# Routing logits of all units by fp32 matmuls from unsplit rows

## The chip, the cores and the metric

The kernel runs on one core of one Trainium2 chip. The metric is the device time of one execution in microseconds (us). Engines are called PE (TensorE, the matmul engine), DVE (VectorE), ACT (ScalarE), POOL (GpSimd) and SP (SyncE, which here issues most of the DMAs).

## The reference

The input x has 8 sequences of 2880 tokens with 192 channels, all fp32. Eight heads of 24 channels each get a causal convolution of 7 taps, whose weights are a softmax over the taps. The 23040 rows that come out go through a mixture of experts in two levels:

```
g_logits = x @ w_group                 # 192 x 4
g_idx = argmax(g_logits);  g_w = softmax(g_logits)[g_idx]
e_logits = x @ w_expert[g_idx]         # 192 x 4 in each group
e_idx = argmax(e_logits);  e_w = softmax(e_logits)[e_idx]
out = g_w * e_w * (relu(x @ w1[g_idx, e_idx]) @ w2[g_idx, e_idx])   # 192 -> 1024 -> 192
```

So each row goes to one of 16 experts, and 20 logits a row (4 for the groups and 16 for the experts) decide which.

## The kernel before

**Units.** The rows are routed in 18 units of 4, 8 or 12 blocks of 120 rows: units 0 to 5 have 4, 8, 12, 8, 8 and 8 blocks, units 6 to 17 have 12 each. A unit is a generator, `unit(u)`, which yields after each small step. `step()` moves one of the two or three live units on by a step, and `gaps(u)` says how many steps lie between the transposes, the logits and the transposes back. A unit does, in this order:

- the convolution as matmuls with a banded matrix (L421), copied from PSUM by ACT into `xc` (L430);
- for each group q of four blocks, transposes of `xc` into PSUM on PE, channels 0 to 127 in `turn_a` (L440) and channels 128 to 191 in `turn_b` (L455), and their copies into the tiles `tah` and `tb`, 480 columns wide;
- `logits()` (L477): matmuls whose moving operand is such a tile and whose stationary is a slice of a zero-padded table of router weights. The groups q write to different rows of one PSUM tile, so all accumulate into it, with all M rows of it each time;
- `logits_back()` (L487): four transposes back, so that rows stand in partitions again, and the copy into `lg`;
- softmax, argmax and prefix sums on DVE (L526 to L556), and the store of the convolved rows to DRAM;
- after `rest` more steps, counts by two small matmuls (L567, L568), places in the experts' lists on DVE (L571 to L607: `ohl`, `ohr`, `ohv`), after up to eight more steps (`LISTLAG`) the list matmuls (L622), and a scatter of row numbers to a table in DRAM (L634).

**Two ways to the logits.** PE multiplies fp32 exactly, or takes fp32r operands, which are fp32 rounded by the engine that writes them. `UF = 7` chooses: units 0 to 6 use fp32 (the table `wrf`, two matmuls for each q, `tah` with 128 channels and `tb` with 64, M = 20 x the number of groups). Units 7 to 17 use fp32r: ACT writes `tah` and the upper half of `tb` rounded (L447, L460), DVE writes what the rounding left into `tal` and into the lower half of `tb` (L448, L461), the table `wrz` holds rounded weights and their rests side by side, so that M is 40 x the number of groups, and there are three matmuls for each q. After the transposes back ACT copies one half and DVE adds the other (L495, L496).

**Experts.** After five units the first portion of the lists is opened, and the experts' slots of 256 rows begin: a gather of rows (L706), transposes (L719, L720), `hidden` (L737, w1, with fp32r operands and their rests), relu into `hh` and `hl` (L742 ACT, L743 DVE), `back` (L755, L759, w2) into two PSUM banks of the pool `po`, and `finish`: the scaling into `ys` (L806 ACT, L807 DVE), which frees the banks, and a scatter into the output (L810). Weights come from DRAM through SP's queue (L655 to L659) into a ring of three buffers and are split into rounded part and rest by ACT and DVE (L671 to L687). The first portion has one slot for each of the 16 experts, the two others two, and 18 tail slots end the program. The steps of units 5 to 17 run between the matmuls of the slots, at a rate worked out from what must be routed before the next portion opens; so the later units stand further apart.

**Order.** A scheduler sets each engine's final order from this program order, except where `keep_in_program_order` holds it. Engines work in order: what waits on DVE holds up what stands behind it there. PSUM has eight banks: three in `pm`, three in `ph`, two in `po`; once the slots run, units use `pm` alone.

Of the kernel before, what the change touches and what calls it, by code (L numbers as in the profile page):

```python
# [35 lines left out]
def conv_moe_kernel(  # L36
# [98 lines left out]
    UF = 7  # L135
# [206 lines left out]
    W2 = 2 * NL  # L342
    QS = UB // QB
    WA = (QS - 1) * W2
    wrz = const.tile([P, 3, WA + QS * W2], F32R, name="wrz")
# [3 lines left out]
    def router_weights():  # L349
        nc.gpsimd.memset(wrf, 0.0)  # L350
        nc.gpsimd.tensor_copy(out=wrf[:, :, WF:WF + NL], in_=wr)
        nc.vector.memset(wrz.bitcast(F32), 0.0)
        nc.vector.tensor_copy(out=wrz[:, 0:2, WA:WA + NL], in_=wr)
        nc.vector.tensor_copy(out=wrz[:, 2, WA:WA + NL], in_=wr[:, 0, :])
        nc.vector.tensor_tensor(
            out=wrz[:, 0:2, WA + NL:WA + W2], in0=wr, in1=wrz[:, 0:2, WA:WA + NL].bitcast(F32), op=ALU.subtract)

# [18 lines left out]
    def unit(u, pre=None):  # L376
# [57 lines left out]
        WQ2 = NL if u < UF else W2  # L434
        parts, lgts = {}, []

        def turn_a(q):
            psa = bank("t")
            for i in range(QB):
                nc.tensor.transpose(psa[:, i * BT:(i + 1) * BT], xc[0:BT, q * QB + i, 0:P], ident[0:BT, 0:BT])  # L440
            tah = pa.tile([P, QN], F32R, name="tah", bufs=QS)
            tal = pa.tile([P, QN], F32R, name="tal", bufs=QS)
            if u < UF:
                nc.scalar.activation(out=tah.bitcast(F32), in_=psa[:, 0:QN], func=AF.Copy)
                parts[q] = (tah.bitcast(F32),)
                return
            nc.scalar.activation(out=tah, in_=psa[:, 0:QN], func=AF.Copy)  # L447
            nc.vector.tensor_tensor(out=tal, in0=psa[:, 0:QN], in1=tah.bitcast(F32), op=ALU.subtract)  # L448
            parts[q] = tah, tal

        def turn_b(q):
            psb = bank("t")
            tb = pa.tile([P, QN], F32R, name="tb", bufs=QS)
            for i in range(QB):
                nc.tensor.transpose(psb[0:D2, i * BT:(i + 1) * BT], xc[0:BT, q * QB + i, P:D], ident[0:BT, 0:BT])  # L455
            if u < UF:
                nc.scalar.activation(out=tb[0:D2].bitcast(F32), in_=psb[0:D2, 0:QN], func=AF.Copy)
                parts[q] += (tb.bitcast(F32),)
                return
            nc.scalar.activation(out=tb[0:D2], in_=psb[0:D2, 0:QN], func=AF.Copy)  # L460
            nc.vector.tensor_tensor(out=tb[D2:P], in0=psb[0:D2, 0:QN], in1=tb[0:D2].bitcast(F32), op=ALU.subtract)  # L461
            parts[q] += (tb,)

        def logits():

            lt = bank("l")
            M = NQ * WQ2
            if u < UF:
                ops = [
                    (wrf[0:n, k, WF - q * NL:WF - q * NL + M], parts[q][k][0:n])  # L470
                    for q in range(NQ) for k, n in enumerate((P, D2))]
            else:
                ops = [
                    (wrz[:, (0, 2, 1)[k], WA - q * W2:WA - q * W2 + M], parts[q][k])
                    for q in range(NQ) for k in range(3)]
# [7 lines left out]
        def logits_back():  # L483
            lgp = bank("l")
            M = NQ * WQ2
# [4 lines left out]
            lgv = lgp[0:BT, 0:QB * M].rearrange("p (i q n) -> p i q n", i=QB, n=WQ2)  # L490
            lgq = lg[0:BT].rearrange("p (q i) n -> p i q n", i=QB)
            if u < UF:
                nc.scalar.activation(out=lgq, in_=lgv, func=AF.Copy)
                return
            nc.scalar.activation(out=lgq, in_=lgv[:, :, :, NL:], func=AF.Copy)  # L495
            nc.vector.tensor_tensor(out=lgq, in0=lgq, in1=lgv[:, :, :, 0:NL], op=ALU.add)  # L496
# [795 lines left out]
```

## Time and profile before

| | us |
|---|---|
| median of 3 runs | 1213.55 (1210.65 to 1219.6) |
| the profiled execution | 1214.05, its span 1212.2 |
| busy: PE | 1129.5 (93%) |
| busy: DVE | 862.2 (71%) |
| busy: ACT | 696.7 (57%) |
| busy: POOL | 495.0 (41%) |
| chain that ended last | PE 66%, DVE 16%, DMA 8%, issue 4%, ACT 4% |

A row of a group names line, engine, operation, output<-inputs, shapes, count, then busy us and mean ns of one, then the idle time just before it on its engine and what ended it. A row of the timeline has the start, the duration (of a merged piece with its count), and in brackets the idle time before and its releaser. A row of the stages has the stretch, its length, the busy us of PE, of PE's weight loads, of DVE, ACT and POOL, then the granted PE clock as a share of full speed, the DMA share and GB/s. Matmul records overlap, so the time that a matmul takes in a stream is read from start to start. An fp32 matmul has two records, an fp32r one has one.

### The profile page before, as it was taken

What the parts mean: (1) busy time and instruction counts of PE and PEld (TensorE: products, weight loads), DVE (VectorE), ACT (ScalarE), POOL (GpSimd) and SP (SyncE); (2) the same over time, 40 slices, a digit from 0 to 9 for tenths busy, and PEclk for the clock granted to TensorE, in tenths of its full rate; (3) what the DMA queues carried; (4) which work ended last, traced back from release to release, by engine and by line L of the source; (5) the groups of instructions that cost most, each with busy time, mean ns of one, the idle gap of its engine ahead of it and who ended that gap; (6) DMA issues with size and microseconds to landing.
All of it is one profiled execution on the core that took longest, in us unless ns stands there. A gap on an engine that the chain in (4) does not pass through costs nothing.

```text
span 1212.2 us, 23621 instructions
## 1 busy us (share of the span) xinstructions
PE 1129.5 (93%) x8219; PEld 1062.1 (88%) x8219; DVE 862.2 (71%) x1835; ACT 696.7 (57%) x1362; POOL 495.0 (41%) x441
## 2 busy tenths in 40 slices
PE   5878899989899999999999999999999999999994
PEld 4444788888899999999999899999999999999994
DVE  4556998898687868676778556666666566687882
ACT  4544566665556556555644445555556555687782
POOL 2003033323334435433343434444444444577771
PEclk9989999999899999999999999999999999999997
DMA  8756588777967464543635657544444456389960
GB/s 210 215 141 153 148 223 191 204 191 195 222 192 213 118 166 137 156 119 104 162 108 145 87 137 212 153 125 137 136 129 136 129 150 162 99 247 258 263 169 15
DMA packets 169628, 195.62 MB, mean 161 GB/s; under 512 B 24932, under 2 KB 146749, under 8 KB 169502
## 3 DMA queue, kind: packets, MB, share of 16 engines
q1 hardware_dynamic: 127454, 140.43, 43.6%
q0 software_dynamic: 18720, 35.83, 10.7%
q10 hardware_dynamic: 23328, 17.80, 6.0%
q8 instruction: 65, 1.06, 0.4%
q14 instruction: 61, 0.50, 0.2%
HBM read 158.80 MB, written 36.58 MB: 161 GB/s over the span
## 4 chain that ended last, share of the span: by engine, by line
PE 66%; DVE 16%; DMA 8%; issue 4%; ACT 4%; SPq 1%; POOL 0%; POOLq 0%; DVEq 0%; ACTq 0%
PE ph L737 28%; PE po L755 17%; PE po L759 8%; PE pm L421 3%; DVE hl L743 3%; DVE ohl L599 2%; PE pm L477 2%; DMA out<-ys,idpt 2%; DMA xin<-in_x 2%; DVE cw L687 1%; DMA raw<-in_moe_w 1%; PE pm L719 1%; PE pm L720 1%; DMA xcd<-xc 1%; DVE tb L461 1%
## 5 line engine op out<-in xcount | busy, mean ns | idle before, releaser
L755 PE MATMUL po<-cw,hh 128*128 128x384 f32 x1424 | 445.8, 371 | 12.2 <-DVE ys L807 12.0
L737 PE MATMUL ph<-xa,ah 128*128 128x256 f32 x1424 | 390.0, 296 | 4.7 <-DVE hl L743 4.6
L810 POOL DMA_INDIRECT out<-ys,idp x160 | 169.2, 1058 | 474.5 <-DVE ys L807 415.4
L759 PE MATMUL po<-cw,hl 128*128 128x192 f32 x1424 | 357.8, 251 | 0.0
L743 DVE SCALAR_TENSOR_TENSOR hl<-ph,hh 128x512 fp32r<-128x512 f32 x356 | 241.2, 685 | 139.8 <-ACT hh L742 137.9
L742 ACT ACTIVATE hh<-ph 128x512 fp32r<-128x512 f32 x356 | 210.6, 593 | 204.1 <-PE ph L737 194.2
L755 PEld LDWEIGHTS po<-cw,hh 128*128 128x128 f32 x1424 | 269.7, 189 | 17.3 <-DVE ys L807 13.9
L737 PEld LDWEIGHTS ph<-xa,ah 128*128 128x128 f32 x1424 | 272.9, 192 | 7.4 <-DVE hl L743 5.0
L759 PEld LDWEIGHTS po<-cw,hl 128*128 128x128 f32 x1424 | 273.8, 192 | 2.0
L706 POOL DMA_INDIRECT xg<-xcd,idp x160 | 186.4, 1165 | 54.6 <-issue 25.9
L737 PE MATMUL ph<-xb,bh 128*128 128x256 f32 x712 | 202.8, 285 | 0.0
L737 PE MATMUL ph<-xb,bl 128*128 128x256 f32 x712 | 202.5, 284 | 0.0
L737 PE MATMUL ph<-xa,al 128*128 128x256 f32 x712 | 202.2, 284 | 0.0
L737 PEld LDWEIGHTS ph<-xa,al 128*128 128x128 f32 x712 | 137.5, 193 | 1.9
L737 PEld LDWEIGHTS ph<-xb,bl 128*128 128x128 f32 x712 | 137.7, 193 | 0.0
L737 PEld LDWEIGHTS ph<-xb,bh 128*128 128x128 f32 x712 | 137.2, 193 | 0.1
L687 DVE TENSOR_TENSOR cw<-rawc,cw 128x768 fp32r<-128x768 f32 x114 | 105.5, 954 | 16.1 <-ACT cw L686 14.0
L725 ACT ACTIVATE xb<-pm 64x256 fp32r<-64x256 f32 x98 | 36.0, 368 | 111.2 <-DVE xa L722 111.2
L672 DVE TENSOR_TENSOR al<-raw,ah 128x1024 fp32r<-128x1024 f32 x57 | 70.6, 1239 | 33.4 <-ACT ah L671 33.4
L686 ACT ACTIVATE cw<-rawc 128x768 fp32r<-128x768 f32 x114 | 90.8, 836 | 3.2 <-DMA rawc<-in_moe_w 3.2
L807 DVE SCALAR_TENSOR_TENSOR ys<-po,xg,ys 128x192 f32<-128x192 f32 x187 | 76.1, 416 | 23.1 <-ACT ys L806 16.7
L806 ACT ACTIVATE ys<-po,xg 128x192 f32<-128x192 f32 x187 | 76.1, 418 | 21.3 <-PE po L759 12.7
(258 smaller groups left out, 1601.4 us busy)
## 6 DMA issues: line engine op xcount, KB each, us to landing
rawc<-in_moe_w SPq DMA_DIRECT2D x114, 384.0 KB
raw<-in_moe_w SPq DMA_DIRECT2D x57, 512.0 KB
raw<-in_moe_w SPq DMA_DIRECT2D x114, 256.0 KB
xcd<-xc ACTq DMA_DIRECT2D x13, 1085.6 KB
xin<-in_x SPq DMA_DIRECT2D x7, 1134.0 KB
xc<-in_moe_w SPq DMA_DIRECT2D x18, 384.0 KB
xin<-in_x SPq DMA_DIRECT2D x6, 1039.5 KB
xin<-in_moe_w SPq DMA_DIRECT2D x9, 512.0 KB
```

The lines of the kernel that those rows point to most:

```text
L672: eng.get(k, nc.vector).tensor_tensor(out=al, in0=ra, in1=ah.bitcast(F32), op=ALU.subtract)
L686: pin(PINW, nc.scalar.activation(out=cw[:, fs, 0, :], in_=rc[k - 2], func=AF.Copy))
L687: eng.get(k, nc.vector).tensor_tensor(out=cw[:, fs, 1, :], in0=rc[k - 2], in1=cw[:, fs, 0, :].bitcast(F32), op=ALU.subtract,)
L706: nc.gpsimd.indirect_dma_start(out=xs[:, t, :], out_offset=None, in_=xcd[0:known, :], in_offset=bass.IndirectOffsetOnAxis(ap=ids[:, t, 0:1 ...
L737: nc.tensor.matmul(out=hp[:, j], lhsT=wgt[:, fs], rhs=xx, start=i == 0, stop=i == len(ops) - 1)
L742: nc.scalar.activation(out=hh, in_=hp, func=AF.Relu)
L743: nc.vector.scalar_tensor_tensor(out=hl, in0=hp, scalar=0.0, in1=hh.bitcast(F32), op0=ALU.max, op1=ALU.subtract,)
L755: nc.tensor.matmul(out=oo[t][:, 0:2 * D], lhsT=hh[:, j, ts], rhs=cw[:, f].rearrange("p a d -> p (a d)"), start=f == 0, stop=False,)
L759: nc.tensor.matmul(out=oo[t][:, 0:D], lhsT=hl[:, j, ts], rhs=cw[:, f, 0, :], start=False, stop=f == NF - 1,)
L806: nc.scalar.activation(out=ys[:, t, :], in_=oo[t][:, D:2 * D], func=AF.Copy, scale=g)
L807: nc.vector.scalar_tensor_tensor(out=ys[:, t, :], in0=oo[t][:, 0:D], scalar=g, in1=ys[:, t, :], op0=ALU.mult, op1=ALU.add,)
L810: nc.gpsimd.indirect_dma_start(out=outviews[nscat[0] % len(outviews)], out_offset=bass.IndirectOffsetOnAxis(ap=ids[:, t, 0:1].bitcast(U32) ...
```

## The change

All units take the fp32 way. `UF`, the table `wrz`, the tiles `tal` and the lower half of `tb` are gone, and so are the rests on DVE and the addition after the transposes back. For units 7 to 17 `logits()` makes six matmuls of fp32 with M = 60 in place of nine of fp32r with M = 120. Nothing else in the source differs.

```diff
--- before.py
+++ after.py
@@ -132,7 +132,6 @@
     FRU = 99
     FRE = nc.gpsimd
     FRH = 0
-    UF = 7
     UG = [0, 5, 3, 6, 1, 4, 0, 8, 0, 5, 3, 6, 0, 4, 4, 7, 0, 5, 4, 6, 2, 6, 5, 10]
     SK = [8, 8, 6, 11, 10, 9, 9]
     KPRE = [5, 6, 16, 33, 35, 47, 63, 68, 79]
@@ -339,21 +338,13 @@
         nc.vector.tensor_scalar(out=band[0:R, h], in0=band[0:R, h], scalar1=wr_[0:R, h:h + 1], scalar2=None, op0=ALU.mult)
 
 
-    W2 = 2 * NL
     QS = UB // QB
-    WA = (QS - 1) * W2
-    wrz = const.tile([P, 3, WA + QS * W2], F32R, name="wrz")
     WF = (QS - 1) * NL
     wrf = const.tile([P, 2, WF + QS * NL], F32, name="wrf")
 
     def router_weights():
         nc.gpsimd.memset(wrf, 0.0)
         nc.gpsimd.tensor_copy(out=wrf[:, :, WF:WF + NL], in_=wr)
-        nc.vector.memset(wrz.bitcast(F32), 0.0)
-        nc.vector.tensor_copy(out=wrz[:, 0:2, WA:WA + NL], in_=wr)
-        nc.vector.tensor_copy(out=wrz[:, 2, WA:WA + NL], in_=wr[:, 0, :])
-        nc.vector.tensor_tensor(
-            out=wrz[:, 0:2, WA + NL:WA + W2], in0=wr, in1=wrz[:, 0:2, WA:WA + NL].bitcast(F32), op=ALU.subtract)
 
 
     posn = const.tile([P, N // BT], I32, name="posn")
@@ -431,48 +422,31 @@
         lg = rt.tile([P, UB, NL], F32, name="lg")[:, 0:nb]
         QN = QB * BT
         NQ = nb // QB
-        WQ2 = NL if u < UF else W2
         parts, lgts = {}, []
 
         def turn_a(q):
             psa = bank("t")
             for i in range(QB):
                 nc.tensor.transpose(psa[:, i * BT:(i + 1) * BT], xc[0:BT, q * QB + i, 0:P], ident[0:BT, 0:BT])
-            tah = pa.tile([P, QN], F32R, name="tah", bufs=QS)
-            tal = pa.tile([P, QN], F32R, name="tal", bufs=QS)
-            if u < UF:
-                nc.scalar.activation(out=tah.bitcast(F32), in_=psa[:, 0:QN], func=AF.Copy)
-                parts[q] = (tah.bitcast(F32),)
-                return
+            tah = pa.tile([P, QN], F32, name="tah", bufs=QS)
             nc.scalar.activation(out=tah, in_=psa[:, 0:QN], func=AF.Copy)
-            nc.vector.tensor_tensor(out=tal, in0=psa[:, 0:QN], in1=tah.bitcast(F32), op=ALU.subtract)
-            parts[q] = tah, tal
+            parts[q] = (tah,)
 
         def turn_b(q):
             psb = bank("t")
-            tb = pa.tile([P, QN], F32R, name="tb", bufs=QS)
+            tb = pa.tile([P, QN], F32, name="tb", bufs=QS)
             for i in range(QB):
                 nc.tensor.transpose(psb[0:D2, i * BT:(i + 1) * BT], xc[0:BT, q * QB + i, P:D], ident[0:BT, 0:BT])
-            if u < UF:
-                nc.scalar.activation(out=tb[0:D2].bitcast(F32), in_=psb[0:D2, 0:QN], func=AF.Copy)
-                parts[q] += (tb.bitcast(F32),)
-                return
             nc.scalar.activation(out=tb[0:D2], in_=psb[0:D2, 0:QN], func=AF.Copy)
-            nc.vector.tensor_tensor(out=tb[D2:P], in0=psb[0:D2, 0:QN], in1=tb[0:D2].bitcast(F32), op=ALU.subtract)
             parts[q] += (tb,)
 
         def logits():
 
             lt = bank("l")
-            M = NQ * WQ2
-            if u < UF:
-                ops = [
-                    (wrf[0:n, k, WF - q * NL:WF - q * NL + M], parts[q][k][0:n])
-                    for q in range(NQ) for k, n in enumerate((P, D2))]
-            else:
-                ops = [
-                    (wrz[:, (0, 2, 1)[k], WA - q * W2:WA - q * W2 + M], parts[q][k])
-                    for q in range(NQ) for k in range(3)]
+            M = NQ * NL
+            ops = [
+                (wrf[0:n, k, WF - q * NL:WF - q * NL + M], parts[q][k][0:n])
+                for q in range(NQ) for k, n in enumerate((P, D2))]
             for i, (wgt, xx) in enumerate(ops):
                 nc.tensor.matmul(
                     out=lt[0:M, 0:QN], lhsT=wgt, rhs=xx, start=i == 0, stop=i == len(ops) - 1)
@@ -482,18 +456,14 @@
 
         def logits_back():
             lgp = bank("l")
-            M = NQ * WQ2
+            M = NQ * NL
             for i in range(QB):
                 nc.tensor.transpose(
                     lgp[0:BT, i * M:(i + 1) * M], lgts[0][0:M, i * BT:(i + 1) * BT], ident[0:M, 0:M],
                 )
-            lgv = lgp[0:BT, 0:QB * M].rearrange("p (i q n) -> p i q n", i=QB, n=WQ2)
+            lgv = lgp[0:BT, 0:QB * M].rearrange("p (i q n) -> p i q n", i=QB, n=NL)
             lgq = lg[0:BT].rearrange("p (q i) n -> p i q n", i=QB)
-            if u < UF:
-                nc.scalar.activation(out=lgq, in_=lgv, func=AF.Copy)
-                return
-            nc.scalar.activation(out=lgq, in_=lgv[:, :, :, NL:], func=AF.Copy)
-            nc.vector.tensor_tensor(out=lgq, in0=lgq, in1=lgv[:, :, :, 0:NL], op=ALU.add)
+            nc.scalar.activation(out=lgq, in_=lgv, func=AF.Copy)
 
         ga, gl, gb, rest = gaps(u)
         events = {}
```

The scheduler's order around it moves a little. On PE, here the logits of unit 9 (`tah`, `tb`, `tal` its transposed tiles, `wrz` and `wrf` the tables), which stand between `back` of one slot and `hidden` of the next. Before:

```order
L759 MATMUL po_1871<-cw_1908,hl_2070 128x192
L477 MATMUL pm_2244<-tah_2033,wrz_200 120x480
L477 MATMUL pm_2244<-tal_2034,wrz_200 120x480
L477 MATMUL pm_2244<-tb_2057,wrz_200 120x480
...
L477 MATMUL pm_2244<-tb_2193,wrz_200 120x480
L737 MATMUL ph_2267<-xa_1978,ah_2046 128x256
...
L737 MATMUL ph_2267<-xb_1979,bl_2074 128x256
L622 LDWEIGHTS ohl_2140
L622 MATMUL pm_2273<-ohv_2142,ohl_2140 128x64
```

Now (lines of the changed kernel: L451 is the logits' matmul, L592 the list's, L707 and L729 those of `hidden` and `back`):

```order
L729 MATMUL po_1826<-cw_1863,hl_2021 128x192
L451 MATMUL pm_2189<-tah_1987,wrf_200 60x480
L451 MATMUL pm_2189<-tb_2009,wrf_200 60x480
...
L451 MATMUL pm_2189<-tb_2139,wrf_200 60x480
L707 MATMUL ph_2209<-xa_1932,ah_1998 128x256
...
L707 MATMUL ph_2209<-xb_1933,bl_2025 128x256
L592 LDWEIGHTS ohl_2088
L592 MATMUL pm_2215<-ohv_2090,ohl_2088 128x64
```

Six matmuls stand where nine stood, and the list of unit 8 still comes after the first five matmuls of `hidden`.

On DVE, at unit 7, the first one that was split. `off` to `pos` begin the list work of unit 5, `mx` and `dd` the softmax of unit 6. Before:

```order
L556 RECIPROCAL xc_858<-se_1191 120x8
L448 TENSOR_TENSOR tal_1227<-pm_1221,tah_1226 128x480
L461 TENSOR_TENSOR tb_1231<-po_1230,tb_1231 64x480
L448 TENSOR_TENSOR tal_1253<-pm_1247,tah_1252 128x480
L461 TENSOR_TENSOR tb_1257<-ph_1256,tb_1257 64x480
L448 TENSOR_TENSOR tal_1276<-po_1270,tah_1275 128x480
L461 TENSOR_TENSOR tb_1280<-pm_1279,tb_1280 64x480
L571 TENSOR_TENSOR off_1290<-ph_1287,eoff_159 128x16
```

Now:

```order
L526 RECIPROCAL xc_843<-se_1171 120x8
L496 TENSOR_REDUCE mx_1296<-lg_1022 120x60
L541 TENSOR_TENSOR off_1261<-ph_1258,eoff_159 128x16
L543 TENSOR_REDUCE mx16_1263<-ph_1258 128x1
L547 TENSOR_TENSOR endr_140<-ph_1258,endr_140 128x16
```

The six rests are gone, and the first reduction of the softmax stands ahead of the list work.

On SP, where the second portion's lists are loaded (`idp1`, sixteen loads, one for each expert; `raw` and `rawc` are weights). Before, from the tenth load on:

```order
L1042 DMA idp1_4122<-idtab_88 128x4
L659 DMA rawc_3618<-in_moe_w2 128x4x192
L659 DMA rawc_3781<-in_moe_w2 128x4x192
L1042 REGISTER_ALU
...
L656 DMA raw_3780<-in_moe_w1 64x1024
L657 DMA raw_3780<-in_moe_w1 64x1024
L655 DMA raw_3961<-in_moe_w1 128x1024
```

Now, from the last of the sixteen on:

```order
L1012 DMA idp1_4021<-idtab_88 128x4
L629 DMA rawc_3521<-in_moe_w2 128x4x192
L629 DMA rawc_3683<-in_moe_w2 128x4x192
L626 DMA raw_3682<-in_moe_w1 64x1024
L627 DMA raw_3682<-in_moe_w1 64x1024
L625 DMA raw_3863<-in_moe_w1 128x1024
```

The weights that stood after ten loads, and after twelve, now stand after all sixteen.

## The prediction

> **What bounds the kernel now.** I read the busy time by stages first, then the waits of TensorE (PE), then single rows. The stages are cut where the kind of work changes: routing alone up to 107 us, the hand-over, expert slots with dense routing, a stretch without logits, expert slots with sparse routing, and the rest.
>
> ```profile
> core 0: us, PE busy (x) PEld busy (x) DVE busy (x) ACT busy (x) POOL busy (x), PEclk, DMA share, GB/s
> 0.00:107.00 107.00, 82.43 (x386) 48.34 (x386) 59.55 (x258) 53.24 (x138) 15.67 (x38) 0.94 0.72 185
> 107.00:131.00 24.00, 16.87 (x98) 11.60 (x98) 20.32 (x78) 8.62 (x22) 7.55 (x8) 0.90 0.62 159
> 131.00:290.00 159.00, 144.82 (x1044) 134.48 (x1043) 140.03 (x322) 98.10 (x198) 46.38 (x41) 0.96 0.72 189
> 290.00:345.00 55.00, 49.82 (x358) 48.18 (x357) 44.51 (x87) 32.65 (x62) 17.69 (x17) 0.94 0.82 205
> 345.00:660.00 315.00, 309.54 (x2374) 302.15 (x2373) 239.21 (x509) 180.06 (x354) 133.52 (x115) 0.99 0.55 150
> 660.00:1212.00 552.00, 525.98 (x3969) 517.33 (x3967) 358.54 (x585) 324.00 (x590) 274.19 (x226) 0.98 0.57 151
> ```
>
> From 345 us on PE is the bound: 309.5 of 315 us. From 131 to 290 us PE (144.8 of 159) and DVE (140.0) are nearly level, and PE loses 14.2 us idle and 4% of its granted clock, 159 x 0.04 = 6.4 us. What ends PE's idle time, for 107 to 131, 131 to 290 and 345 to 660 us in turn:
>
> ```profile
> PE pm L622 <- DVE ohv L607: 7.1, 4, 3.9
> ...
> PE pm L622 <- DVE ohv L607: 10.4, 7, 3.1
> PE pm L622 <- DVE tal L448: 1.4, 1, 1.4
> ...
> PE po L755 <- DVE ys L807: 5.4, 5, 2.0
> ```
>
> PE waits for DVE each time. So the change has two hands: it makes PE slower and DVE freer.
>
> **PE's cost.** Units 7 to 17, eleven of them, now do nine f32r matmuls of 480 columns each; the changed kernel does six fp32 ones, as units 0 to 6 do already. Unit 6 shows the price: five fp32 matmuls (two records each) start to start from 104.19 to 108.91 us. The chain has one unit's nine f32r ones whole.
>
> ```profile
> 104.19 1.01 PE L477 MATMUL ph<-tb,wrf 64*60 64x480 f32 x2
> 107.97 1.01 PE L477 MATMUL ph<-tb,wrf 64*60 64x480 f32 x2
> 108.91 0.63 PE L440 MATMUL pm<-ident,xc 120*128 120x120 f32 x4
> ...
> 348.73 1.98 PE pm L477 x9
> 621.01 1.97 PE pm L477 x9
> ```
>
> An fp32 matmul takes 4.72 / 5 = 0.944 us, six take 5.66; nine f32r ones take 1.97. That is +3.69 us a unit, +40.6 us for eleven, before anything is hidden. (The Trainium skill, "FP8 and Floating Point Precision", section TensorE Precision Notes, says that true FP32 is four passes through the array; this trace's f32r matmul, 1.97 / 9 = 0.219 us, times four is 0.876, and 0.944 was measured. By the page the sum would be 11 x 0.41 = 4.5 us smaller. The measured row decides.) The four transposes back (L487) get 60 columns instead of 120 and the copy and the transposes before the logits keep their sizes: nothing, because each is a few hundredths of a us.
>
> **DVE's relief.** Per unit three rest tiles tal, three tb, and one addition go:
>
> ```profile
> L448 DVE TENSOR_TENSOR tal<-pm,tah 128x480 fp32r<-128x480 f32 x32 | 20.9, 652 | 8.4 <-ACT tah L447 8.3
> L461 DVE TENSOR_TENSOR tb<-pm,tb 64x480 fp32r<-64x480 f32 x31 | 20.2, 651 | 1.8 <-ACT tb L460 0.7
> L496 DVE TENSOR_TENSOR lg<-lg,pm 120x240 f32<-120x240 f32 x11 | 4.4, 401 | 2.0 <-ACT lg L495 1.9
> ```
>
> 6 x 0.65 + 0.40 = 4.3 us a unit, 47 us in all. ScalarE loses nothing: it made its f32r copies by instructions of the same size.
>
> **Before 107 us: 0.** The four wrz instructions on DVE go, but the first matmuls wait for x, at 14.51 us, not for DVE, and what comes later there is paced by transfers (DMA share 0.72, PE 82 of 107 us).
>
> ```profile
> 14.51 1.60 PE L421 MATMUL ph<-xin,band 126*120 126x192 f32 x4 [1.10 <-DMA xin<-in_x]
> ```
>
> **107 to 131 us, unit 7: -3 us.** DVE does not rest from 110.24 us until after 131 (20.3 of 24 us busy, 3.75 idle ahead of that row), and PE stands for its lists.
>
> ```profile
> 110.24 0.66 DVE L448 TENSOR_TENSOR tal<-pm,tah 128x480 fp32r<-128x480 f32 x1 [3.75 <-ACT tah L447]
> 112.98 0.18 DVE L571 TENSOR_TENSOR off<-ph,eoff 128x16 f32<-128x16 f32 x1
> 127.92 0.56 DVE L607 TENSOR_TENSOR ohv<-ohr,vals 120x384 bf16<-120x384 bf16 x1
> ...
> 118.38 0.35 PE L622 MATMUL pm<-ohv,ohl 120*128 120x64 bf16 x6 [3.92 <-DVE ohv L607]
> 128.53 0.35 PE L622 MATMUL pm<-ohv,ohl 120*128 120x64 bf16 x6 [2.27 <-DVE ohv L607]
> ```
>
> Four rest tiles lie between 110.24 and 112.98, 2.7 us, and the addition is 0.4: the lists are done 3.1 us sooner. PE's 3.69 us fall into the 3.92 us in which it stood. If the cover is gone it costs the whole 3.7; if PE's clock recovers too (0.90 over 24 us, 2.4 us), it is -5. I take -3.
>
> **131 to 290 us, units 8 to 12: +2 us.** Here I must say how much of PE's loss goes. All six rest tiles of a unit stand on DVE ahead of the list for which PE stands; for unit 10:
>
> ```profile
> 199.47 0.65 DVE L448 TENSOR_TENSOR tal<-pm,tah 128x480 fp32r<-128x480 f32 x1
> 209.55 0.65 DVE L461 TENSOR_TENSOR tb<-pm,tb 64x480 fp32r<-64x480 f32 x1
> 213.47 0.55 DVE L607 TENSOR_TENSOR ohv<-ohr,vals 120x384 bf16<-120x384 bf16 x1
> ...
> 214.07 0.35 PE L622 MATMUL pm<-ohv,ohl 120*128 120x64 bf16 x6 [3.07 <-DVE ohv L607]
> ```
>
> Without them (3.9 us) this 3.07 us wait would be over. For unit 9 the logits stand ahead of the list in PE's order, so DVE also gets 3.69 us more. PE's pure work becomes 144.8 - 6.4 + 5 x 3.69 = 156.9 us. DVE's becomes 140.0 - 5 x 4.3 = 118.5, a share of about 0.74 of the new stage. From 345 to 660 us DVE's share is 0.76, and PE loses 5.5 us idle and 1% of clock, 8.6 of 315 us or 2.7%. With that rate the stage takes 156.9 / 0.973 = 161.2 us, +2.2. Bounds: no loss left, -2.1; all of it kept, +18.5.
>
> **290 to 345 us: 0.** No logits fall here. A weight transfer that takes 10.96 us ends PE's wait, by way of DVE. In the new order SyncE issues all sixteen loads of the second portion's list before the next weights, where ten, two and four were mixed with weights before; six loads at 0.49 us are 3 us later. DVE's earlier splits free weight buffers sooner. Bounds -5 (the 5.2 us of idle time) and +3; I take 0 between them.
>
> ```profile
> 284.80 4.89 SPq L1042 DMA_DIRECT2D idp<-idtab  x10
> ...
> 310.58 10.96 DMA raw<-in_moe_w
> ...
> 324.58 0.58 PE L737 MATMUL ph<-xa,ah 128*128 128x256 f32 x1 [2.90 <-DVE hl L743]
> ```
>
> **345 to 660 us, units 13 to 17: +14 us.** PE is full, so 5 x 3.69 = 18.45 us stand on the path. The waits left are for po banks, which ys frees behind DVE's list work; for unit 17:
>
> ```profile
> 607.94 0.65 DVE L448 TENSOR_TENSOR tal<-pm,tah 128x480 fp32r<-128x480 f32 x1
> 608.97 0.74 DVE L807 SCALAR_TENSOR_TENSOR ys<-po,xg,ys 128x192 f32<-128x192 f32 x2
> ...
> 609.44 0.44 PE L755 MATMUL po<-cw,hh 128*128 128x384 f32 x1 [1.98 <-DVE ys L807]
> ```
>
> One or two rest tiles (0.6 to 1.3 us) go from such a wait of up to 2.0. I take half of the stage's 8.6 us loss: 18.45 - 4.3 = +14.1. Bounds +9.8 and +18.5. After 660 us nothing changes but its start.
>
> **Sum.** 0 - 3 + 2.2 + 0 + 14.1 = +13.3 us. The profiled execution took 1214.05 us (span 1212.2 and 1.85 around it), so 1227.4; the median of the runs shown is 0.5 lower, so **1227 us**.
>
> **Rivals.**
> *No relief.* PE's waits end on ohv and ys, not on tal and tb, and the lists are long by themselves (two ohl of 0.95 us); if the scheduler fills DVE's free time with other work ahead of them, PE pays in full outside unit 7: 10 x 3.69 = +37, 1250 us. For it: only 3.5 us of PE's waits end on a rest tile itself. Against it: the rest tiles stand right ahead of those lists.
> *DVE was the bound up to 345 us.* Then its relief there pays for PE's work: -5 in unit 7's stretch, -2.1, -5, and +9.8 later make -2, 1211 us, not slower than before. For it: 140 of 159 us busy, and weights are loaded when DVE frees their buffers. Against it: PE's own floor of 156.9 us, which no relief can lower, and the +9.8. It decides if PE's idle time from 131 to 290 us falls below 1 us.
> *The clock does not come back.* PE's idle time goes, yet the granted clock stays low in these stages, for PE's load and not its rests set it: 6.4 us and the 2.4 of unit 7's stretch stay, +9, 1236 us. The low clock lies where PE stood twice for 1.3 us:
>
> ```profile
> 180.00:190.00 10.00, 7.39 (x49) 6.47 (x48) 9.23 (x20) 6.04 (x12) 5.87 (x5) 0.83 0.53 139
> 181.52 0.35 PE L622 MATMUL pm<-ohv,ohl 120*128 120x64 bf16 x6 [1.33 <-DVE ohv L607]
> 183.15 0.34 PE L622 MATMUL pm<-ohv,ohl 120*128 120x64 bf16 x6 [1.28 <-DVE ohv L607]
> ```
>
> (The Trainium skill, "TensorE: Matmul & The Clock Gate", section What's actually happening, wants an idle window of about 3.4 us for the clock to fall. Two rests of 1.3 us make no such window, so the trace does not agree here; by the page something else lowers the clock, which is this rival.)
>
> **How the numbers follow.** The forecast (1220 to 1236) gets 0.50, no relief 0.15, DVE as the bound (1208 to 1220) 0.25, the clock 0.07, and 0.03 is left for an order that hides more than all waits known. A measurement of this kernel tells about 1%, 12 us, from no change: above 1225.7 is slower. Of the forecast's 0.50, 0.31 lie above; with 0.15, 0.07 and 0.01 slower is 0.54. Faster than 1201 would need more than every wait above: 0.03. The rest, 0.43, is the same. The range goes from 1215, above most of the DVE rival, to 1244, short of no relief at all.
>
> **What would show it.** L477's successor should show 12 records a unit at about 0.58 us, and six matmuls in 5.6 to 5.7 us on the chain. DVE's busy time should fall from 862 to about 815 us. From 131 to 290 us the same work should take about 161 us with PE's waits for ohv at a third of 10.4 us, and from 345 to 660 us about 329. It is wrong if the fp32 matmuls go faster than 0.9 us between experts' matmuls, if the waits for ohv stay, or if the weights after the list loads come late.

## The result and the profile after

On the chip of the first measurement the changed kernel took 1233.28 us in the median of six runs (1230.31 to 1249.03), the kernel before beside it 1215.64. The run of 1249.03 us is a slow one, and the ratio is of the other five. It is 1.0138, 95% interval 1.0101 to 1.0175: slower, by less than 2%. Measured twice more on other chips the ratio was 1.0198 (1.0148 to 1.0248) and 1.0211 (1.0161 to 1.026), so the first figure is the low one of three. On the base of the prediction, 1213.55 us, the three make 1230.3, 1237.6 and 1239.2 us, against a forecast of 1227 (1215 to 1244). The profiled execution took 1230.69 us (span 1229.0), 16.6 us more than that of before.

The page of after, its busy line and the shares of its chain by engine (before: PE 1129.5 and DVE 862.2 us; chain PE 66%, DVE 16%):

```profile
PE 1165.0 (95%) x8252; PEld 1050.9 (86%) x8252; DVE 816.3 (66%) x1754; ACT 699.0 (57%) x1362; POOL 495.1 (40%) x441
...
PE 76%; DMA 8%; DVE 7%; issue 3%; ACT 3%; SPq 1%; POOL 1%; POOLq 0%; DVEq 0%; ACTq 0%
```

DVE lost 46 us of work, and its share of the chain fell by 9 points; PE's rose by 10. The chain of after shows what a unit's six matmuls took (12 records, start and duration), here for units 10, 13 and 17; all eleven units show 5.66 or 5.67:

```profile
214.41 5.66 PE pm L451 x12
...
353.03 5.67 PE pm L451 x12
...
636.43 5.66 PE pm L451 x12
```

To see where the time came from I cut both traces at the same work, not at the same time: at the first logits matmul of units 7, 8, 12, 13 and 17 (unit 7's stand at 111.2 us in before, behind the prediction's cut at 107). The stages of after, and of before with that cut (columns as in the prediction):

```profile
0.00:113.50 113.50, 89.79 (x413) 52.65 (x414) 57.02 (x253) 56.07 (x143) 19.61 (x42) 0.89 0.74 186
113.50:149.50 36.00, 31.98 (x217) 24.96 (x217) 30.83 (x110) 17.23 (x40) 5.90 (x6) 0.95 0.54 143
149.50:277.20 127.70, 124.14 (x827) 99.43 (x827) 97.38 (x235) 80.16 (x162) 39.71 (x34) 1.00 0.78 193
277.20:353.00 75.80, 68.81 (x474) 62.40 (x474) 54.45 (x103) 42.17 (x80) 28.10 (x24) 0.95 0.79 197
353.00:636.40 283.40, 282.73 (x2058) 257.94 (x2057) 186.45 (x385) 158.96 (x311) 110.03 (x99) 1.00 0.52 142
636.40:1229.00 592.60, 567.56 (x4271) 553.52 (x4270) 390.17 (x673) 344.43 (x629) 291.74 (x241) 0.99 0.56 151
```

```profile
0.00:111.20 111.20, 86.63 (x413) 50.75 (x413) 60.47 (x260) 55.30 (x143) 18.96 (x41) 0.94 0.73 189
111.20:151.10 39.90, 30.54 (x217) 26.20 (x216) 36.77 (x120) 18.81 (x43) 5.27 (x6) 0.91 0.50 131
151.10:276.10 125.00, 113.06 (x816) 104.52 (x815) 112.59 (x262) 78.53 (x159) 41.30 (x36) 0.97 0.78 202
276.10:348.70 72.60, 67.42 (x471) 64.84 (x470) 58.27 (x109) 42.41 (x80) 23.71 (x21) 0.93 0.78 200
348.70:621.00 272.30, 268.36 (x2046) 261.90 (x2045) 203.23 (x414) 157.47 (x311) 114.10 (x98) 0.99 0.54 147
621.00:1212.20 591.20, 563.46 (x4268) 553.88 (x4266) 390.82 (x674) 344.14 (x629) 291.67 (x241) 0.99 0.57 151
```

Row by row the lengths differ by +2.3, -3.9, +2.7, +3.2, +11.1 and +1.4 us, 16.8 in all. Each row but the first begins with the logits of the unit at which it is cut, so the third holds those of units 8 to 11, the fourth those of unit 12, the fifth those of units 13 to 16 and the last those of unit 17. Unit 12's logits took 5.66 us in after; the chain of before has

```profile
276.06 3.22 PE pm L477 x9
```

where the nine f32r matmuls ran at a low clock for the most part, so 2.4 of the fourth row's +3.2 are unit 12's own. In the third row PE's busy time rises by 11.1 us (124.14 against 113.06), the stage only by 2.7: PE's idle time falls from 11.9 to 3.6 us. In the fifth row PE had 3.9 us idle to give and has 0.7 left, so 11.1 us of the 14.8 (four units at 3.69) stand there in full. The waits of PE say what idle time went; after, for 113 to 149, 149 to 277, 277 to 353 and 353 to 637 us in turn (total, times, longest):

```profile
PE pm L592 <- DVE ohv L577: 3.3, 2, 2.4
...
PE pm L592 <- DVE ohv L577: 2.3, 2, 1.6
PE po L725 <- DVE ys L777: 1.1, 1, 1.1
...
PE ph L707 <- DVE hl L713: 5.0, 1, 5.0
...
PE po L725 <- DVE ys L777: 0.6, 1, 0.6
```

The wait for ohv in units 8 to 12 was 10.4 us and is 2.3; that for ys in units 13 to 17 was 3.9 with this cut and is 0.6. The wait for hl falls in the fourth row, where a weight transfer comes late by way of DVE: 2.9 before, 5.0 now.

### The profile page after: what moved, and what is told of

Read it like the earlier page. It is cut to its first block, busy times and chain, and to the rows that moved or that the text cites. A ratio compares the mean times of both kernels' runs of the same rounds, so it can differ in the third digit from the quotient of the medians.

```text
span 1229.0 us, 23613 instructions
## 1 busy us (share of the span) xinstructions
PE 1165.0 (95%) x8252; PEld 1050.9 (86%) x8252; DVE 816.3 (66%) x1754; ACT 699.0 (57%) x1362; POOL 495.1 (40%) x441
## 3 DMA queue, kind: packets, MB, share of 16 engines
q0 software_dynamic: 18720, 35.83, 10.4%
## 4 chain that ended last, share of the span: by engine, by line
PE 76%; DMA 8%; DVE 7%; issue 3%; ACT 3%; SPq 1%; POOL 1%; POOLq 0%; DVEq 0%; ACTq 0%
PE ph L707 30%; PE po L725 19%; PE po L729 9%; PE pm L451 5%; PE pm L412 3%; DMA xg<-xcd,idpt 2%; DMA out<-ys,idpt 2%; DMA xin<-in_x 2%; PE pm L689 1%; PE pm L690 1%; DVE hl L713 1%; PE pm L430 1%; DMA raw<-in_moe_w 1%; DMA rawc<-in_moe_w 1%; DVE ohl L569 1%
## 5 line engine op out<-in xcount | busy, mean ns | idle before, releaser
L707 PE MATMUL ph<-xa,ah 128*128 128x256 f32 x1424 | 389.3, 295 | 5.3 <-DVE hl L713 5.2
L729 PE MATMUL po<-cw,hl 128*128 128x192 f32 x1424 | 357.8, 251 | 0.0
L780 POOL DMA_INDIRECT out<-ys,idp x160 | 165.8, 1036 | 475.3 <-DVE ys L777 420.2
L725 PEld LDWEIGHTS po<-cw,hh 128*128 128x128 f32 x1424 | 269.2, 189 | 18.8 <-DVE ys L777 11.1
L707 PEld LDWEIGHTS ph<-xa,ah 128*128 128x128 f32 x1424 | 272.1, 191 | 10.6 <-DVE hl L713 5.2
L729 PEld LDWEIGHTS po<-cw,hl 128*128 128x128 f32 x1424 | 273.8, 192 | 1.8
L676 POOL DMA_INDIRECT xg<-xcd,idp x160 | 189.5, 1185 | 54.0 <-issue 29.3
L707 PE MATMUL ph<-xb,bh 128*128 128x256 f32 x712 | 202.2, 284 | 0.0
L707 PE MATMUL ph<-xb,bl 128*128 128x256 f32 x712 | 202.2, 284 | 0.0
L707 PE MATMUL ph<-xa,al 128*128 128x256 f32 x712 | 201.8, 284 | 0.0
L707 PEld LDWEIGHTS ph<-xa,al 128*128 128x128 f32 x712 | 137.1, 193 | 1.8
L707 PEld LDWEIGHTS ph<-xb,bl 128*128 128x128 f32 x712 | 137.1, 193 | 0.0
L707 PEld LDWEIGHTS ph<-xb,bh 128*128 128x128 f32 x712 | 136.6, 192 | 0.0
```

The lines of the kernel that those rows point to most:

```text
L676: nc.gpsimd.indirect_dma_start(out=xs[:, t, :], out_offset=None, in_=xcd[0:known, :], in_offset=bass.IndirectOffsetOnAxis(ap=ids[:, t, 0:1 ...
L707: nc.tensor.matmul(out=hp[:, j], lhsT=wgt[:, fs], rhs=xx, start=i == 0, stop=i == len(ops) - 1)
L725: nc.tensor.matmul(out=oo[t][:, 0:2 * D], lhsT=hh[:, j, ts], rhs=cw[:, f].rearrange("p a d -> p (a d)"), start=f == 0, stop=False,)
L729: nc.tensor.matmul(out=oo[t][:, 0:D], lhsT=hl[:, j, ts], rhs=cw[:, f, 0, :], start=False, stop=f == NF - 1,)
L780: nc.gpsimd.indirect_dma_start(out=outviews[nscat[0] % len(outviews)], out_offset=bass.IndirectOffsetOnAxis(ap=ids[:, t, 0:1].bitcast(U32) ...
```

## The experiments

The theory to test: PE pays 3.69 us in each of eleven units, DVE is freed of 4.3 us in each, and the second covers the first where PE waits for DVE's lists (units 7 to 12) and not where PE is full (units 13 to 17). The rivals were: no relief; DVE as the bound of the dense part, which would make the relief worth as much as the cost; and a clock that does not come back.

**The relief alone (first form).** Units 7 to 17 stay with f32r; the rest tiles and the addition are not made. What it leaves out are the products with the rests of the rows.

```diff
-            nc.vector.tensor_tensor(out=tal, in0=psa[:, 0:QN], in1=tah.bitcast(F32), op=ALU.subtract)
-            parts[q] = tah, tal
+            parts[q] = tah, tah
...
-            nc.vector.tensor_tensor(out=tb[D2:P], in0=psb[0:D2, 0:QN], in1=tb[0:D2].bitcast(F32), op=ALU.subtract)
...
-                    (wrz[:, (0, 2, 1)[k], WA - q * W2:WA - q * W2 + M], parts[q][k])
-                    for q in range(NQ) for k in range(3)]
+                    (wz[:, 0:M] if k == 1 else wrz[0:n, (0, 2, 1)[k], WA - q * W2:WA - q * W2 + M], parts[q][k][0:n])
+                    for q in range(NQ) for k, n in enumerate((P, P, D2))]
```

> The kernel before, with PE's nine f32r matmuls a unit kept, but without DVE's part in units 7 to 17: no rest tiles and no addition. It leaves out the products with the rests (the second matmul of each q multiplies the rounded tile by zeros, the third takes 64 channels). Theory (DVE's relief is what gave time back): the 40.6 us that PE paid less the 16.8 us by which the profiled execution grew is about 24 us, and it should show here alone: 15 to 27 us less than before, ratio 0.978 to 0.988, with PE's waits for ohv from unit 7 to unit 12 under a third of what they were. Rival (the time came from the longer logits, which give DVE time ahead of the lists): less than 5 us, ratio above 0.995.

Measured: 1219.87 us, ratio 1.0007 (0.998 to 1.0034). That looked like no relief at all, but it was no clean test: the third matmul of each q now had 64 rows. The timeline of this kernel, PE, unit 9 (start, duration):

```profile
180.08 0.39 PE L476 MATMUL pm<-tah,wrz 128*120 128x480 f32 x1
180.31 0.37 PE L476 MATMUL pm<-tah,wz 128*120 128x480 f32 x1
180.62 0.48 PE L476 MATMUL pm<-tb,wrz 64*120 64x480 f32 x1
181.03 0.48 PE L476 MATMUL pm<-tah,wrz 128*120 128x480 f32 x1
```

From start to start 0.23 us between two matmuls of 128 rows, and 0.31 and 0.41 where 128 and 64 rows follow on each other. Nine took 2.90 to 2.92 us in place of 1.97, and unit 10's took 5.06 at a granted clock of 0.50 (in before 3.6, at 0.60 on average and with the matmuls of a list among them). That is some 11 us over eleven units (ten times 0.93 and once about 2), which hid what DVE gave.

**The relief alone, all matmuls with 128 rows.** As above, with the lower half of `tb` left in place as zeros that are written once:

```diff
+    tbz = [const.tile([P, QB * BT], F32R, name=f"tbz{q}") for q in range(QS)]
+        for t in tbz:
+            nc.gpsimd.memset(t.bitcast(F32), 0.0)
...
-            tb = pa.tile([P, QN], F32R, name="tb", bufs=QS)
+            tb = pa.tile([P, QN], F32R, name="tb", bufs=QS) if u < UF else tbz[q]
```

> As the first experiment (no rest tiles and no addition on DVE in units 7 to 17, the products with the rests left out), but all nine f32r matmuls keep stationaries of 128 rows: the third one's tile has zeros in its lower half. In the first experiment the third matmul took 64 rows, and nine matmuls took 3.0 us in place of 1.97, which by itself is 11 us over eleven units. Theory (relief gives time, and that 11 us hid it): nine matmuls in 1.97 us, 8 to 19 us less than before, ratio 0.984 to 0.993. Rival (without PE's extra work DVE's relief is worth nothing, since something else, weights or the clock, sets the pace of the dense stage): ratio 0.997 to 1.003.

Measured: 1201.82 us against 1213.54, ratio 0.9908 (0.9874 to 0.9942). Nine f32r matmuls take 1.95 to 1.97 us again, and the 1.0% between this kernel and the one above, 12 us, is near those 11. Its stages, unit 8's to unit 12's logits and unit 13's to unit 17's:

```profile
150.50:266.20 115.70, 109.18 (x816) 101.92 (x815) 97.29 (x234) 79.54 (x163) 41.61 (x34) 1.00 0.86 212
338.20:605.50 267.30, 266.57 (x2047) 260.05 (x2046) 186.26 (x385) 158.64 (x311) 110.30 (x98) 1.00 0.56 149
```

The first is 9.3 us shorter than in before (125.0), with the clock at 1.00 in place of 0.97; the second 5.0 us (272.3). So the relief is real, and of what these two stages show two thirds lie in the dense part.

**The cost alone.** The changed kernel, where DVE still makes the rest tiles and one more operation of the addition's size; nothing reads the rests.

```diff
+            if u >= 7:
+                tal = pa.tile([P, QN], F32R, name="tal", bufs=QS)
+                nc.vector.tensor_tensor(out=tal, in0=psa[:, 0:QN], in1=tah, op=ALU.subtract)
...
+            if u >= 7:
+                nc.vector.tensor_tensor(out=tb[D2:P], in0=psb[0:D2, 0:QN], in1=tb[0:D2], op=ALU.subtract)
...
+            if u >= 7:
+                nc.vector.tensor_tensor(out=lgq, in0=lgq, in1=lgv, op=ALU.max)
```

> The changed kernel with DVE's work put back: in units 7 to 17 DVE still computes the rest tiles, which nobody reads, and takes a maximum of the logits with themselves in place of the addition. Theory: PE's 3.69 us a unit come nearly unpaid, 10 or 11 times, 33 to 41 us over before, ratio 1.027 to 1.034, with the waits for ohv back except where the longer logits cover them. Rival (the longer logits give DVE the time, not its relief): as the changed kernel, ratio 1.012 to 1.016.

Measured: 1252.97 us against 1218.3, ratio 1.0295 (1.0245 to 1.0346), +36 us. Its stage from unit 8's to unit 12's logits:

```profile
148.70:287.40 138.70, 131.65 (x826) 101.22 (x825) 111.61 (x263) 79.33 (x160) 42.44 (x36) 0.95 0.69 182
```

So 36 of the 40.6 us of PE's cost come. The stage takes 138.7 us, against 125.0 before and 127.7 in after, but these do not compare directly: unit 10's logits ran at half clock here, 10.7 us in place of 5.66. The second measurement of the whole change (below) has the same in unit 10, and there the stage took nearly as long:

```profile
146.85:283.63 136.78, 132.52 (x827) 102.34 (x826) 97.46 (x234) 80.05 (x162) 39.13 (x34) 0.94 0.72 180
```

Between these two DVE's work makes 1.9 us of the stage. The waits for ohv in it did not come back whole either:

```profile
PE pm L599 <- DVE ohv L584: 4.7, 2, 3.1
```

They were 10.4 us before and are 2.6 in the second measurement, so the longer logits by themselves close more than half of them, as the prediction had said of unit 9. Where DVE's work shows more is from unit 6's to unit 8's logits (49.3 us here, 44.8 in the second measurement) and from unit 13's to unit 17's (288.4 and 283.6). These are single executions. The two halves, 0.9908 and 1.0295, add up to 1.020, which is what the second and third measurement of the whole change gave: the relief is worth about 11 us with PE's added work as without it.

**Unit 7 to fp32 and the others not.** Before with one number changed:

```diff
-    UF = 7
+    UF = 8
```

> The kernel before with units 0 to 7 by fp32 (one unit more) and units 8 to 17 as before. Theory: from unit 7's logits to unit 8's the changed kernel took 36.0 us where before took 39.9, so this should be 3 to 4 us faster than before, ratio 0.997, which is at the edge of what five rounds tell. Rival (unit 7's gain was unit 8's relief): no gain, or up to 3.7 us slower.

Measured: ratio 1.0002 (0.9975 to 1.0029). The prediction had -3 us for this unit by itself, and the 3.9 us that after shows there had seemed to bear it out. They do not: in this kernel the way from unit 6's logits to unit 8's takes 50.5 us, against 48.4 in before and 44.6 in after. One row of its timeline tells why (PE, a transpose of unit 8):

```profile
146.82 0.60 PE L455 MATMUL pm<-ident,xc 120*64 120x120 f32 x4 [2.85 <-DVE tb L461]
```

PE waits 2.85 us for a rest tile of unit 8, which DVE makes only after unit 7's lists. The waits for ohv did fall, from 7.1 to 4.4 us between the logits of units 7 and 8, but this wait takes their place. What after gains there is unit 8's relief, not unit 7's.

**The late units to fp32, and 7 to 12 not.**

```diff
-    UF = 7
+    FU = tuple(range(7)) + tuple(range(13, 18))
...
-            if u < UF:
+            if u in FU:
```

> The kernel before with fp32 in units 13 to 17 beside 0 to 6, and the split way in units 7 to 12. Theory: PE is full there, five units at 3.69 us less little relief, 12 to 15 us slower than before, ratio 1.010 to 1.012: most of the whole change's loss. Rival (the loss is spread evenly over eleven units): 5/11 of 16.8, 7.6 us, ratio 1.006.

Measured: ratio 1.0147 (1.0101 to 1.0193), with 283.9 us from unit 13's to unit 17's logits (after 283.4, before 272.3). That is a little above the 1.010 to 1.012 foretold, which the interval reaches, and clear of the rival's 1.006: five units make most of the whole change's loss.

**The dense units to fp32, and 13 to 17 not.** Measured on one chip, and profiled once more on another.

```diff
-    UF = 7
+    UF = 13
```

> The kernel before with fp32 in units 0 to 12, the split way in units 13 to 17: the other half of the fourth experiment. Theory: in the dense stage PE's 3.69 us a unit are paid back by DVE's relief almost whole, 0 to 6 us over before, ratio 1.000 to 1.005, so that this and the late units add up to the whole change. Rival (the loss is even over the units): 6/11 of 16.8 is 9 us, ratio 1.0075.

> The kernel of the sixth experiment (fp32 in units 0 to 12) profiled once more. There unit 10's six fp32 matmuls ran at a granted clock of 0.50 and took 10.70 us in place of 5.66. Theory (which logits fall into a low clock is chance): another execution has that at another unit or nowhere, and is 4 to 9 us shorter if nowhere. Rival (this order always brings it there): unit 10 again at about 10.7 us.

Measured: ratio 1.0067 (1.0042 to 1.0093), 1222.27 us over ten runs between 1216 and 1228; the one run on the other chip took 1229.45. I had expected about nothing, and the time alone fits the rival, an even loss (1.0075). Together with the late units' 1.0147 it makes 1.021. The chain of the first trace has unit 10's logits, six matmuls, at nearly twice their time, and its stages give the clock, 0.50 behind the busy times of the five engines:

```profile
212.85 10.70 PE pm L477 x12
```

```profile
213.00:220.00 7.00, 7.00 (x9) 0.96 (x9) 0.28 (x2) 0.00 (x0) 1.00 (x1) 0.50 0.55 118
220.00:227.00 7.00, 7.00 (x15) 3.68 (x16) 0.42 (x1) 1.49 (x4) 0.95 (x1) 0.50 0.00 0
```

From unit 8's to unit 12's logits this kernel took 135.3 us, where after took 127.7 with the same fp32 units; 7.2 us of the difference lie between unit 10's and unit 11's logits. So the loss is not even over the units. The second profile has the same 10.70 us in the same unit, as the rival of that experiment had it: for this kernel two executions of two.

**The change twice more.** The changed kernel itself, on two other chips:

> The changed kernel once more, unaltered, for a narrower interval and a second profile beside the halves. If the halves add up (late units 1.0147, dense units 1.0067) it should come at 1.018 to 1.021; if the dense units' loss is mostly chance of the clock, at 1.012 to 1.016 as the first time.

> The changed kernel as it is, beside the next one on the same chip. Both theories: a ratio to the kernel before of 1.012 to 1.022. In the profile unit 10's logits take 5.66 us (full clock) or 10.70 us (half clock); with 10.70 the way from unit 10's logits to unit 11's is about 36.8 us, with 5.66 about 29.1.

Measured: 1.0198 and 1.0211, as above; the first is what the halves add up to. The first of the two again has unit 10's logits at half clock. Its timeline on PE ahead of them, its stages from there on, and then the same place in after:

```profile
210.83 0.35 PE L592 MATMUL pm<-ohv,ohl 120*128 120x64 bf16 x6 [1.84 <-DVE ohv L577]
...
212.28 0.34 PE L592 MATMUL pm<-ohv,ohl 120*128 120x64 bf16 x6 [0.76 <-DVE ohv L577]
...
213.16 1.86 PE L451 MATMUL pm<-tah,wrf 128*60 128x480 f32 x2
```

```profile
213.20:218.50 5.30, 5.30 (x7) 0.78 (x6) 0.60 (x3) 0.00 (x0) 1.00 (x1) 0.50 0.52 114
218.50:224.00 5.50, 5.50 (x8) 0.96 (x7) 0.00 (x0) 0.03 (x1) 0.00 (x0) 0.50 0.00 0
224.00:228.00 4.00, 4.00 (x13) 3.45 (x13) 0.67 (x2) 2.08 (x5) 1.26 (x2) 0.50 0.00 1
228.00:234.00 6.00, 6.00 (x38) 5.20 (x36) 4.59 (x9) 4.39 (x9) 3.06 (x3) 0.87 0.65 192
```

```profile
212.28 0.35 PE L592 MATMUL pm<-ohv,ohl 120*128 120x64 bf16 x6 [1.58 <-DVE ohv L577]
...
213.73 0.33 PE L592 MATMUL pm<-ohv,ohl 120*128 120x64 bf16 x6 [0.76 <-DVE ohv L577]
...
214.34 1.02 PE L451 MATMUL pm<-tah,wrf 128*60 128x480 f32 x2
```

With nearly the same waits ahead, one execution goes through unit 10 at full clock and the other at half. From unit 10's logits to unit 11's it takes 36.8 us there and 29.1 in after, 7.7 us more. In the third measurement the same six matmuls took

```profile
215.59 6.76 PE pm L451 x12
```

so they were slow in part, which is neither of the two figures foretold. Fp32 logits of unit 10 were at half clock for all of their time in four executions (the cost alone, the dense units twice, the change again), for a part in three, and at full clock in two: after, and the next kernel. The fall itself is no work of the change: in before the clock was at 0.50 from 215.0 to 218.4 us, within unit 10's f32r logits.

**The rest ahead of the lists filled.** The changed kernel, with eight fp32 matmuls whose result nothing reads ahead of the list matmuls of units 7 to 12:

```diff
         pl = bank("l")
+        for _ in range(KW if 7 <= u <= 12 else 0):
+            nc.tensor.matmul(out=pl[:, 256:384], lhsT=ident, rhs=ident, start=True, stop=True)
```

> For units 7 to 12 eight fp32 matmuls of 128 columns, whose result nothing reads, stand in PE's order ahead of the list matmuls, where PE waits for ohv. Theory (the clock falls in unit 10 because PE rests 1.8 and 0.8 us just ahead of its logits, in some executions and not in others): the rest ahead of unit 10's list falls below 0.6 us, its logits take 5.66 us, and the median lies 3 to 6 us (0.25 to 0.5%) below the changed kernel's of the same chip. Rival (the fall does not hang on that rest): no gain or a loss of up to 2 us, since the matmuls themselves take PE 0.2 us each and stand where PE waits; 10.70 us in the profile would say so too.

Measured: 1247.99 us, ratio 1.0219 (1.0183 to 1.0256), against 1.0211 for the change on the same chip. The timeline on PE and the stages around unit 10:

```profile
218.01 1.97 PE L592 MATMUL pm<-ident 128*128 128x128 f32 x16
219.93 0.34 PE L595 MATMUL pm<-ohv,ohl 120*128 120x64 bf16 x6
221.39 0.33 PE L595 MATMUL pm<-ohv,ohl 120*128 120x64 bf16 x6 [1.12 <-DVE ohv L578]
...
222.28 1.02 PE L452 MATMUL pm<-tah,wrf 128*60 128x480 f32 x2
```

```profile
185.00:222.00 37.00, 35.88 (x259) 29.61 (x259) 28.51 (x67) 20.99 (x44) 10.58 (x9) 1.00 0.82 196
222.00:251.00 29.00, 29.00 (x185) 22.98 (x185) 17.88 (x42) 18.34 (x39) 10.52 (x9) 1.00 0.76 191
```

In the profile the theory's sign is there: the wait ahead of unit 10's first list is gone (one of 1.12 us ahead of its second is left), and unit 10's logits run at full clock. The time is not: no gain. The added matmuls are six times 1.97 us, 11.8 us of PE work, of which the waits for ohv give back 3.6 (7.0 us from 110 to 290 us in the trace of the change beside it, 3.4 here); the other 8 us are more than the clock's fall costs. Since this kernel was profiled in one execution only, and after too had been at full clock there with its wait, this is a hint that the rests bring the fall, and not proof.

**Fp32 matmuls all with 128 rows.** In the changed kernel `tb` keeps 64 rows of zeros below its channels, so that all six matmuls have 128 rows; first with one fixed tile for each q, then with the three tiles in turn as the pool gave them.

```diff
+    tbz = [const.tile([P, QB * BT], F32, name=f"tbz{q}") for q in range(QS)]
...
-            tb = pa.tile([P, QN], F32, name="tb", bufs=QS)
+            tb = tbz[q]
...
-                (wrf[0:n, k, WF - q * NL:WF - q * NL + M], parts[q][k][0:n])
-                for q in range(NQ) for k, n in enumerate((P, D2))]
+                (wrf[:, k, WF - q * NL:WF - q * NL + M], parts[q][k])
+                for q in range(NQ) for k in range(2)]
```

In the second, `tb = tbz[ntb[0] % QS]` with a counter.

> The changed kernel with the second fp32 matmul of each q on 128 rows in place of 64 (zeros in the lower half of tb and of its weights), so that all stationaries have the same rows. Theory from the first experiment (a load of a stationary with other rows than the matmul in flight does not hide): an fp32 matmul falls from 0.944 us to between 0.82 and 0.88, six take 5.0 to 5.3 us, and the kernel is 3 to 6 us faster than the changed one, ratio to before 1.009 to 1.012. Rival (0.944 is what fp32 takes): 5.66 us as before, ratio 1.012 to 1.016.

> The seventh experiment with its tiles for channels 128 to 191 taken in turn, as the kernel's own ring does, so that a unit no longer writes over the tile of the one before it. Theory: six fp32 matmuls in 4.97 us in place of 5.66, in a stage where PE is full; 5 late units give 3.4 us back surely, all eleven 7.6 at most, ratio to before 1.006 to 1.011 where the changed kernel has 1.014. Rival (the start's shorter matmuls and the dense stage give nothing, and the seventh run's 1.0185 was no accident of its tiles): 1.014 or more.

Measured: 1.0185 (1.0137 to 1.0233) and 1.016 (1.0117 to 1.0203). Both give wrong output, and why stays open, so they are read for what the matmuls take and are no version to use. The timeline of the first, PE, unit 13:

```profile
355.50 1.02 PE L456 MATMUL pm<-tah,wrf 128*60 128x480 f32 x2
356.35 0.97 PE L456 MATMUL pm<-tbz,wrf 128*60 128x480 f32 x2
357.15 0.97 PE L456 MATMUL pm<-tah,wrf 128*60 128x480 f32 x2
357.96 0.97 PE L456 MATMUL pm<-tbz,wrf 128*60 128x480 f32 x2
```

From the first to the fourth start 2.46 us, 0.82 for one, where unit 6 of before gave 0.944 with 128 and 64 rows in turn. Six take 4.97 us on the chain in place of 5.66. From unit 13's to unit 17's logits it takes 280.55 us in place of 283.4: four times 0.7. The second lies 0.4% below the changed kernel of its chip, which the two intervals do not tell apart. So the matmuls got shorter as foretold, and the times foretold with that (1.006 to 1.012) were not reached.

No version that makes the whole computation was faster than before. Making the rests on another engine was not tried.

## Why the prediction was right, and where it was off

**PE's price: right.** Six fp32 matmuls at 5.66 us were read off unit 6, and all eleven units of after show it. The sign of the result hangs on this term and on the full PE of the late units.

**DVE's relief: right in size.** 862 became 816 us (815 foretold). The relief alone is worth 0.9%, 11 us; the forecast had hidden 40.6 - 13.3 = 27 us of the cost behind DVE's waits, a larger figure. The halves tell what hides it: the cost alone leaves 36 of the 40.6 us, so the longer logits hide about 5 by themselves, a half clock in unit 10 included, and the relief gives its 11 beside them. The second and third measurement leave 24 and 26 us, so 15 to 17 are hidden; the 24 of the first are the most favourable of the three.

**Unit 7: the sum near, the step wrong.** It said -3 and the stage shows -3.9, but unit 7 alone gains nothing, so the agreement is luck. The rest tiles that matter there are unit 8's, made behind unit 7's lists on DVE.

**Units 8 to 12: right in sign, near where the clock holds.** The forecast's +2.2 counts five units, the third row's +2.7 only four; with the fourth row, which holds unit 12's logits, it is +5.9 in after. From unit 7's to unit 13's logits, a stretch for which -0.8 was foretold (-3, +2.2 and 0), it is +2.0. The waits for ohv went from 10.4 to 2.3 us, which is what the mechanism asks: PE's added work falls where PE stood. But the cost alone has half of that fall too, so the longer logits close these waits as well as DVE's relief does; how the two share the stage at full clock was not measured. And the execution that after profiled is a favourable one. The dense units alone cost 0.67%, 8 us; a half clock in unit 10, worth up to 7.7 us, accounts for most of that where it falls.

**The clock: its chance was set too low.** The rival said that the granted clock would stay low in these stages, for 9 us and 1236 us in all. In after the clock of the stage rose from 0.97 to 1.00. But in the second measurement it was 0.94, below before, and in seven of nine executions with fp32 logits in unit 10 it was low there, all or part of the way through them; the second and third measurement, 1237.6 and 1239.2, lie near the rival's figure. That the profiled execution of after met a full clock is luck, and so is part of the nearness of its stages to the forecast's; the other runs of that measurement were not profiled. The reason offered for the rival, PE's load, is not what was found: fp32 logits ran at full clock in units 8, 9, 11 and 13 to 17 of every trace that has them there, and in unit 12 in all but one (6.97 us, the cost alone). What was not seen ahead is that the six matmuls make a fall dearer: at half clock they lose 5.0 us where nine f32r ones lost about 2 (4.2 us in unit 10 of the kernel with only the late units as fp32, all at 0.50, of which 0.4 are a list's matmuls).

**Stretch without logits: 0 foretold.** The fourth row's +3.2 contains unit 12's logits, which are 2.4 longer; 0.8 us is left, within what single executions differ by. With unit 12 by fp32r the row took 72.0 to 73.7 us in the traces, with fp32 74.3 to 77.4. The wait for hl behind a weight transfer grew from 2.9 to 5.0 us, in the direction that the list loads' place had given for the upper bound (+3), but the kernel with only the dense units as fp32 had 1.6 and 3.9 us of it; no run undid the order of the loads, so whether it matters stays open.

**Units 13 to 17: right in kind, a little high or low by the run.** +14.1 foretold; the traces give +11.1 for four units in full, and the fifth's 3.7 lies in the tail. The late units alone measured +1.47%, 18 us.

**The first 113 us and the tail: 0 foretold.** They came out at +2.3 and +1.4. Neither can be told from the spread of single executions: from unit 17's logits to the end it took 591.0 to 597.1 us in the traces with unit 17 by fp32r, and 592.6 to 599.9 in those with fp32, whose logits there are 3.0 to 3.7 us longer. The second measurement's trace has 599.7, and there PE stands 3.8 us for hl behind weights that came late. Why some executions have that wait stays open.

**The rivals.** No relief falls by 0.9908 and by 1.0295 against 1.0138 to 1.0211. DVE as the bound falls: the idle time of PE from unit 8 to unit 12 was 3.6 us in after and 4.3 in the second measurement, above the 1 us from which that rival would decide, and PE's added work shows from unit 13 to unit 17, where PE is full. The change measured three times lies 1.4 to 2.1% above before. The forecast's 1.1% was low; of what the second and third lie above it, the traces show the clock in unit 10 (7.7 and 1.1 us more than in after) and the tail (7.1 and 6.1).

## What to carry to other kernels

When work goes from one engine to another, cut both traces at the same piece of work and price it by stage: it is cheap only where the engine that gets it was waiting for the one that loses it. Look at a term by itself before believing that it was right, since here a stage agreed to 1 us for another unit's reason. And where the clock falls in one execution and not in the next, a single profile is one draw: profile it again before pricing a stage to 1%, and compare a stage between two kernels only where its granted clock agrees.

## What the runs showed of the hardware

- **Rows of the stationary.** Matmuls of 128 rows follow each other by 0.22 us (f32r, 480 columns) and 0.82 us (fp32). Where 128 and 64 rows take turns, it is 0.31 to 0.41 and 0.94. A smaller matmul made the row of matmuls longer.
- **Fp32 passes.** With 128 rows throughout an fp32 matmul took 0.82 to 0.83 us, 3.7 to 3.8 times the 0.219 of an f32r one. The Trainium skill, "FP8 and Floating Point Precision", section TensorE Precision Notes, says four passes, and these runs come near to that. The prediction's row of 0.944 us is 0.12 longer, and that goes with the change of rows.
- **The clock's fall and return.** In the second measurement it fell after two rests of 1.84 and 0.76 us with 0.7 us of work between them, and it stayed at 0.50 through 10.7 us of fp32 matmuls without a gap; back at full it was at 229.6 us, 5.7 us after the last of them (0.87 over 228 to 234 us). So it was low for 17.1 us there, and for 3.4 in unit 10 of before with its short f32r matmuls. The Trainium skill, "TensorE: Matmul & The Clock Gate", section What's actually happening, states idle and busy windows of about 3.4 us that run free of the kernel. That the window runs free would agree with a fall that comes in one execution and not in the next; ahead of the fall shown here no single idle window is that long, and 10.7 us of work did not bring the clock back.
